# Order of the first loads and of the decay table in a fused retention and MoE kernel

## The chip, the cores and the metric

One Trainium2 chip, of which the kernel uses one core. The metric is the device time of one execution in microseconds, lower is better. A run is timed several times, and the median stands for it.

## What is computed

Three layers follow one another on 1536 rows (2 sequences of 768 tokens) of 512 numbers, all in float32:

- retention with 8 heads of 64 and one decay lam per head. In words: out[i] is the sum over j <= i of lam^(i-j) (q_i . k_j) v_j within a sequence. The reference works in blocks with a masked product inside a block and a state carried between blocks;
- a first MLP: `relu(x @ w_in)^2 @ w_out`, 512 to 2048 to 512;
- a second, gated MLP: `(sigmoid(x @ w_gate) * (x @ w_val)) @ w_out`, 512 to 1536 to 512.

## The kernel before

**Retention.** The sequences are cut into 12 chunks of 128 tokens (6 per sequence), which are worked in the order `ORDER` (L20). For each chunk, `att_scores` (L258) multiplies q and k on TensorE into PSUM; `att_prep` (L269) lets GpSimd (POOL) make `kd`, the keys times their decay, and from a sequence's second chunk on `qd`, the queries times the rows L, and lets VectorE (DVE) multiply the scores with the decay mask D into `at`, in two halves; `att_out` (L301) gives TensorE the state update (kd by v), the product with `at` (at by v), and the part from the carried state (qd by S); `att_state` (L335) and `att_x` (L347) take the results out on ScalarE (ACT) and VectorE. `att_decay` (L293) makes the decayed state on POOL.

**The decay table.** `powers` (L203) loads lam, lets POOL raise it to the powers 1 to 128 (W, L217), and stores a row of zeros with a one (Z) and then W into a small DRAM tensor `w_dram` over the scalar queue. `decays` (L223) reads that tensor back with shifted and overlapping addresses as the mask D (512 KB, in pieces of 512 bytes) and the rows L (two transfers of 128 KB), over the sync queue (SP). The last column of D is also the key decay that `kd` uses (L281).

**Weights.** Each weight unit (512 KB as it lies in DRAM) is loaded raw (`load_w`, L130), turned by ScalarE (`conv_act`, L140, two activations) and VectorE (`conv_dve`, L155, three operations) into float32, and stored back to DRAM for later. Each `conv_act` also issues the load of one more raw unit. A float32 product is made as three products of a high and a low part, for which `split_w` (L366) makes `whi` on ScalarE and `wlo` on VectorE.

**Order of the work.** Everything is written out by hand: each engine executes its instructions in program order, and waits between engines and for transfers are semaphores. The program loads FIRST, SIDE (over the scalar queue) and EARLY, in which "q0" is q and k of the first chunk in order, "v0" its k and v for the other products, "w" a raw weight unit and "D" the decay table. Then it issues the scores of the first UP = 4 chunks, prepares chunk 0 and runs a loop of LEAD = 7 passes (L815 to L833):

```python
for k, c in enumerate(order[:lead]):
    att_out(c)
    if UP <= k + 3 < lead:
        att_scores(order[k + 3])
    load(LOOP[k])
    ops = conv_dve()
```

A pass then prepares chunk k+1 and takes out chunk k, with the operations of one conversion woven between, and issues CONVS[k] calls of `conv_act`. After the passes `step_1` (L758) runs 16 times: a unit of the first MLP on the first 512 rows (`stage_a`, L406, through `mm_in`, and `stage_b`, L432, through `mm_out`), with up to PACE[f] conversions and the other five chunks in between. The rest of the kernel (the other 1024 rows by a Strassen scheme, and the second MLP) isn't touched. `warm_up` (L236) gives TensorE 44 small products at the start.

Of the kernel before, what the change touches and what calls it, by code (L numbers as in the profile page):

```python
# [7 lines left out]
F32 = mybir.dt.float32  # L8
# [4 lines left out]
P = 128  # L13
CH = 128
# [4 lines left out]

ORDER = (0, 6, 1, 2, 7, 3, 8, 4, 9, 5, 10, 11)  # L20
LEAD = 7
UP = 4
SLOTS = ((1, 3), (5, 8), (11, 13), (16, 19), (22, 25))


FIRST = "q0 q1 v0"
SIDE = "q2 q3"
EARLY = "D v1 w q4"
LOOP = ("v2 v3 q5", "q6 v4 v5 w", "v6 w v7", "q7", "", "", "")
RAW_BUFS = 4  # L30

CONVS = (1, 0, 1, 1, 1, 1, 0)
PACE = (2, 2, 2, 2, 2, 2, 2, 2, 2, 2, 2, 2, 2, 2, 1, 0)

MM = 0.2267
# [5 lines left out]
def retention_moe_kernel(  # L41
# [88 lines left out]
    def load_w(n):  # L130
        for _ in range(min(n, len(to_load))):
            ph, f, u = key = to_load.pop(0)
            t = wp.tile([P, 512, 2], I32, tag="w", name="raw")
            src = (w1 if ph == 1 else w2)[f, u].bitcast(I32)
            nc.sync.dma_start(out=t, in_=src.rearrange("p (n two) -> p n two", two=2))
            raw_t[key] = t

    ready = []

    def conv_act():  # L140

        if not to_conv or to_conv[0] not in raw_t:
            return
        key = to_conv.pop(0)
        t = raw_t.pop(key)
        j = unit("j")
        r = unit("r", I32)
        nc.scalar.activation(j, t[:, :, 1].bitcast(F32), AF.Copy, scale=2.0**-112)  # L150
        nc.scalar.activation(r, t[:, :, 0].bitcast(mybir.dt.uint32), AF.Copy, scale=2.0**-29)  # L151
        ready.append((key, j.bitcast(I32), r))
        load_w(1)

    def conv_dve():  # L155

        if not ready:
            return []
        key, j, r = ready.pop(0)
        ph, f, u = key  # L160
        m = unit("m", I32)
        w = unit("u")
        if ph == 1:
            w_t[key] = w

        def last():
            nc.vector.tensor_tensor(out=w.bitcast(I32), in0=m, in1=r, op=ALU.add)  # L167
            n_stored[0] += 1
            at(clock[0] + 4.0, lambda: nc.sync.dma_start(out=w32[ph][f, u], in_=w))

        return [
            lambda: nc.vector.tensor_scalar(
                out=m, in0=j, scalar1=3, scalar2=None, op0=ALU.logical_shift_left
            ),
            lambda: nc.vector.scalar_tensor_tensor(  # L175
                out=m, in0=j, scalar=-(2**31), in1=m, op0=ALU.bitwise_and, op1=ALU.bitwise_or
            ),
            last,
        ]
# [8 lines left out]
    def run(ops):  # L188
        weave(ops, [])
# [9 lines left out]
    L = const.tile([P, 4, CH], F32, name="L")  # L199
    S = [const.tile([P, 4, 64], F32, name=f"S{i}", tag=f"S{i}") for i in range(2)]  # L200
    w_dram = dram.tile([H, 256], F32, name="w_dram")

    def powers():  # L203


        src = bass.AP(lam.tensor, lam.offset, [[1, H], [0, 16], [1, 1]])
        nc.sync.dma_start(out=lam_sb, in_=src)
        nc.vector.memset(warm, 0.0)
        nc.gpsimd.iota(exi, pattern=[[1, 8]], base=0, channel_multiplier=8)
        nc.vector.memset(Z[:, 0:127], 0.0)  # L210
        nc.vector.memset(Z[:, 127:128], 1.0)
        nc.vector.tensor_scalar(
            out=exi, in0=exi, scalar1=127, scalar2=None, op0=ALU.bitwise_and
        )
        nc.vector.tensor_scalar(out=ex, in0=exi, scalar1=1.0, scalar2=None, op0=ALU.add)
        nc.scalar.dma_start(out=w_dram[:, 0:128], in_=Z)
        nc.gpsimd.tensor_tensor(out=W, in0=lam_sb.to_broadcast([P, 8]), in1=ex, op=ALU.pow)  # L217
        dst = w_dram[:]
        nc.scalar.dma_start(
            out=bass.AP(dst.tensor, dst.offset + 128, [[256, H], [8, 16], [1, 8]]), in_=W  # L220
        )

    def decays():  # L223


        src = w_dram[:]
        nc.sync.dma_start(
            out=D, in_=bass.AP(src.tensor, src.offset, [[1, P], [256, H], [1, CH]])
        )
        for r in range(2):  # L230
            nc.sync.dma_start(
                out=L[64 * r : 64 * r + 64],
                in_=bass.AP(src.tensor, src.offset + 256 * r + 128, [[0, 64], [512, 4], [1, CH]]),
            )
# [14 lines left out]
    def new_xr():  # L249
        for t in (1, 2):  # L250
            xr[t] = xp.tile([P, 4, TB], F32, tag=f"xr{t}", name=f"xr{t}")
# [17 lines left out]
    def att_prep(c):  # L269
        n = c % SEQ_CH  # L270
        sc = sc_t.pop(c)
        at_t[c] = double("at")
        dst = [pv(at_t[c][:, r, :]) for r in range(2)]
        qt = qk_t.pop(c)[:, 0, :]
        kn = kv_t[c][:, 0, :]
        if n < SEQ_CH - 1:
            kd = kd_t[c] = unit("kd")
            nc.gpsimd.tensor_tensor(  # L278
                out=kd.rearrange("s (h d) -> s h d", h=H),
                in0=kn.rearrange("s (h d) -> s h d", h=H),  # L280
                in1=D[:, :, CH - 1 : CH].to_broadcast([P, H, 64]), op=ALU.mult,  # L281
            )
        if n > 0:
            qd = qd_t[c] = unit("qd")
            nc.gpsimd.tensor_tensor(out=pv(qd), in0=pv(qt), in1=L, op=ALU.mult)  # L285
        return [
            lambda r=r: nc.vector.tensor_tensor(
                out=dst[r], in0=pv(sc[r]), in1=Dv[:, r], op=ALU.mult
            )
            for r in range(2)  # L290
        ]
# [431 lines left out]
    def load(what, eng=nc.sync):  # L723

        for x in what.split():
            if x == "w":
                load_w(1)
            elif x == "D":
                decays()
            elif x[0] == "q":  # L730
                load_qk(order[int(x[1:])], eng)
            else:
                load_kv(order[int(x[1:])], eng)
# [70 lines left out]

    with tc.manual_schedule():
        powers()
        load(FIRST)
        load(SIDE, nc.scalar)
        warm_up()
        load(EARLY)  # L810
        new_xr()
        for k in range(UP):
            att_scores(order[k])
        run(att_prep(order[0]))
# [6 lines that stand above are left out]
            if k + 1 < lead:  # L821
                weave(att_prep(order[k + 1]), ops[:2])
                run(att_state(c))
                att_decay(order[k + 1])
                weave(ops[2:], att_x(c))
            else:
                weave(split_w(1, 0), ops)
                rest.append(c)
            for m in range(CONVS[k]):
                if m:  # L830
                    run(conv_dve())
                conv_act()
            flush()  # L833


        keys = [(1, i, 0) for i in range(NF1 // 2)]
        prepare_a(keys[0], T1)
        at(T1 - 20.0, lambda: load_a((1, 1, 0)))
        combine_x([T1 + d for d in (-30, -25, -15, -13, -11, -9, -7, 2, 4, 6, 8)])
        for f in range(NF1):  # L840
            step_1(f)
        n_out = 24
        for k in range(n_out):
            convert(T2 + 1.0 + k * (T3 - T2 - 4.0) / n_out)
        for f in range(NF1):
            prepare_out(1, f, T2 + 24 * MM * f)
        uses = [use for i in range(NF1 // 2) for use in pair_in_1(i)]
        strassen(keys, uses, (None, lambda: close(1)))
        xc.clear()
        new_xr()  # L850
        for f in range(2):
            at(T3 - 24.0 + f, lambda f=f: load_units(2, f))
        at(T3 - 14.0, lambda: run(split_w(2, 0)))
        pair_out(1)


        for f in range(2, NF2):
            at(T3 + (36 * (f - 1) - 12) * MM - 8.0, lambda f=f: load_units(2, f))
        for k in range(3 * NF2 - n_out):
            convert(T3 + 2.0 + 3.6 * k)  # L860
        keys = [(2, i, u) for i in range(NF2 // 2) for u in range(2)]
        prepare_a(keys[0], T4)
        at(T4 - 20.0, lambda: load_a((2, 0, 1)))
        combine_x([T4 - 46.0 + 3.5 * k for k in range(11)])
        for f in range(NF2):
            step_2(f)
        for f in range(NF2):
            prepare_out(2, f, T5 + 24 * MM * f)
        uses = [use for i in range(NF2 // 2) for use in pair_in_2(i)]
        strassen(keys, uses, (None, lambda: close(2)))  # L870
        pair_out(2)
        flush()
        assert not agenda and not to_conv and not ready
# [62 lines left out]
```

## Time and profile before

| | |
|---|---|
| median of 3 runs | 601.86 us (600.67 to 604.19) |
| span of the profiled execution | 599.4 us; the page has no other time of it |
| TensorE busy | 582.6 us, 97% of the span, 3076 matmuls |
| VectorE busy | 448.6 us, 75% |
| ScalarE busy | 332.5 us, 55% |
| POOL busy | 36.9 us, 6% |
| DMA | 127.19 MB, mean 212 GB/s |
| granted TensorE clock | 0.993 of full speed, mean |

The span goes from the first to the last instruction. The profile names engines PE (TensorE matmul), PEld (its weight loads, beside PE), DVE, ACT, POOL and SP; a "q" behind the name (SPq, ACTq) is the sequencer that issues transfers. DMA queue q1 holds the transfers that SP issues, q10 those that ScalarE issues; both run on the same 16 DMA engines. In a timeline, "[0.40 <-DVE wlo L374]" says that the engine stood for 0.40 us before the instruction, until line 374's result was there. Work on an engine that is not the bottleneck costs nothing as long as it is done in time.

### The profile page before, as it was taken

To read this page: it belongs to the slowest core of one execution; us is meant where nothing else is said; L and a number is where in the kernel's file an instruction comes from. 1 tells how busy PE (TensorE), PEld (TensorE's weight loads), DVE (VectorE), ACT (ScalarE), POOL (GpSimd) and SP (SyncE) were. 2 spreads that over 40 slices of the span, in tenths; PEclk is the share of its full clock that TensorE was granted. 3 is DMA by queue.
4 is the path that set the end of the run, shared out by engine and by line. 5 is a ranking of instruction groups with operands and counts; after the bars stand their busy time and mean duration, and the time that the engine had idled before them with its cause. 6 is when DMAs were issued, how large, how long until landed. Compare 5 with 4: busy or idle time off the path is not lost.

```text
span 599.4 us, 8496 instructions
## 1 busy us (share of the span) xinstructions
PE 582.6 (97%) x3076; PEld 478.8 (80%) x3076; DVE 448.6 (75%) x673; ACT 332.5 (55%) x525; POOL 36.9 (6%) x34
## 2 busy tenths in 40 slices
PE   7799999999899999999999999999999999999997
PEld 7677878887678888888888888888888888888885
DVE  0699998999888868988877788694778787569101
ACT  0367787988556456756557654554464455537101
POOL 1672212100000000000000000000000000000000
PEclk9899999999999999999999999999999999999999
DMA  7996898682145377999978945511332422658003
GB/s 212 402 418 232 306 309 331 237 297 87 57 121 208 107 240 271 408 414 415 410 276 279 312 170 172 163 50 54 122 106 106 140 81 80 209 187 357 0 1 141
DMA packets 53578, 127.19 MB, mean 212 GB/s; under 512 B 5784, under 2 KB 7584, under 8 KB 53536
## 3 DMA queue, kind: packets, MB, share of 16 engines
q1 hardware_dynamic: 52376, 124.41, 57.9%
q10 hardware_dynamic: 1160, 2.24, 1.1%
q8 instruction: 24, 0.39, 0.3%
q14 instruction: 18, 0.15, 0.1%
HBM read 90.96 MB, written 35.66 MB: 211 GB/s over the span
## 4 chain that ended last, share of the span: by engine, by line
PE 87%; DVE 4%; DMA 2%; POOL 2%; issue 2%; ACT 1%; SPq 0%; ACTq 0%; POOLq 0%; DVEq 0%
PE p L545 30%; PE p L695 25%; PE p L386 17%; PE p L400 12%; DMA kv<-in_kv 1%; POOL kd L278 1%; PE p L329 1%; PE p L322 1%; POOL qd L285 1%; DMA lam_sb<-in_lam 1%; PE p L264 1%; DVE wlo L374 1%; DVE al L526 1%; DVE m L175 1%; ACT ah L520 1%
## 5 line engine op out<-in xcount | busy, mean ns | idle before, releaser
L545 PE MATMUL p<-xcl,ah 128*128 128x512 f32 x280 | 109.1, 390 | 2.5 <-DVE xcl L469 2.5
L545 PE MATMUL p<-xch,ah 128*128 128x512 f32 x280 | 109.4, 391 | 0.4 <-ACT s L554 0.2
L545 PE MATMUL p<-xch,al 128*128 128x512 f32 x280 | 109.0, 389 | 0.0
L695 PE MATMUL p<-g2h,whi 128*128 128x512 f32 x224 | 87.1, 389 | 0.0
L695 PE MATMUL p<-g2l,whi 128*128 128x512 f32 x224 | 87.1, 389 | 0.0
L695 PE MATMUL p<-g2h,wlo 128*128 128x512 f32 x224 | 87.1, 389 | 0.0
L545 PEld LDWEIGHTS p<-xcl,ah 128*128 128x128 f32 x280 | 52.6, 188 | 13.5 <-DVE xcl L469 2.9
L545 PEld LDWEIGHTS p<-xch,ah 128*128 128x128 f32 x280 | 52.5, 188 | 12.9 <-ACT s L554 1.4
L545 PEld LDWEIGHTS p<-xch,al 128*128 128x128 f32 x280 | 52.6, 188 | 11.0
L559 DVE TENSOR_TENSOR c<-p,s 128x512 f32<-128x512 f32 x60 | 41.2, 688 | 25.3 <-PE p L545 21.4
L554 ACT COPY s<-p 128x512 f32<-128x512 f32 x60 | 35.0, 586 | 37.4 <-PE p L545 37.4
L167 DVE CUSTOM_DVE_ANT_0 u<-m,r 128x1024 uint16<-128x1024 uint16 x68 | 49.5, 728 | 2.7
L374 DVE TENSOR_TENSOR wlo<-u,whi 128x512 fp32r<-128x512 f32 x68 | 46.1, 707 | 7.0 <-ACT whi L372 5.7
L150 ACT ACTIVATE j<-raw 128x512 f32<-128x512 f32 x68 | 45.6, 671 | 10.2 <-issue 5.3
L175 DVE SCALAR_TENSOR_TENSOR m<-j,m 128x512 int32<-128x512 int32 x68 | 49.5, 728 | 1.2
L151 ACT ACTIVATE r<-raw 128x512 int32<-128x512 uint32 x68 | 45.2, 665 | 8.7 <-PE p L695 5.5
L695 PEld LDWEIGHTS p<-g2l,whi 128*128 128x128 f32 x224 | 42.0, 188 | 8.8
L695 PEld LDWEIGHTS p<-g2h,whi 128*128 128x128 f32 x224 | 42.0, 188 | 8.7
L695 PEld LDWEIGHTS p<-g2h,wlo 128*128 128x128 f32 x224 | 42.0, 188 | 8.7
L372 ACT CAST whi<-u 128x512 fp32r<-128x512 f32 x68 | 39.0, 616 | 13.7 <-DVE u L167 13.2
L386 PE MATMUL p<-xh,wlo 128*128 128x512 f32 x160 | 43.2, 392 | 1.1 <-DVE wlo L374 1.1
L386 PE MATMUL p<-xh,whi 128*128 128x512 f32 x160 | 43.8, 395 | 0.0
(87 smaller groups left out, 911.6 us busy)
## 6 DMA issues: line engine op xcount, KB each, us to landing
raw<-in_w SPq DMA_DIRECT2D x68, 512.0 KB, 7.1
w<-u SPq DMA_DIRECT2D x68, 256.0 KB, 4.0
u<-w SPq DMA_DIRECT2D x64, 256.0 KB, 5.5
g<-g SPq DMA_DIRECT2D x56, 256.0 KB, 4.4
g<-g SPq DMA_DIRECT2D x28, 512.0 KB, 7.5
a<-w SPq DMA_DIRECT2D x20, 512.0 KB, 4.3
kv<-in_kv SPq DMA_DIRECT2D x12, 512.0 KB, 8.6
qk<-in_qk SPq DMA_DIRECT2D x10, 512.0 KB, 5.7
```

Of the source, the lines that this page charges most:

```text
L150: nc.scalar.activation(j, t[:, :, 1].bitcast(F32), AF.Copy, scale=2.0**-112)
L151: nc.scalar.activation(r, t[:, :, 0].bitcast(mybir.dt.uint32), AF.Copy, scale=2.0**-29)
L167: nc.vector.tensor_tensor(out=w.bitcast(I32), in0=m, in1=r, op=ALU.add)
L175: lambda: nc.vector.scalar_tensor_tensor(out=m, in0=j, scalar=-(2**31), in1=m, op0=ALU.bitwise_and, op1=ALU.bitwise_or),
L372: nc.scalar.copy(hi, src)
L374: lambda lo=lo, src=src, hi=hi: nc.vector.tensor_tensor(out=lo, in0=src, in1=hi, op=ALU.subtract)
L386: nc.tensor.matmul(acc, lhsT=a[:, kk * P : (kk + 1) * P], rhs=b[:, kk, :], start=i == 0, stop=i == 11,)
L400: nc.tensor.matmul(acc[e], lhsT=a[:, e * P : (e + 1) * P], rhs=b, start=first and i == 0, stop=last and i == 2,)
L545: nc.tensor.matmul(acc, lhsT=w[:, col, kk * P : (kk + 1) * P], rhs=x[:, kk, :], start=start and i == 0, stop=stop and i == 5, skip_group_c ...
L554: nc.scalar.copy(s, acc)
L559: nc.vector.tensor_tensor(out=c, in0=acc, in1=s, op=ALU.add)
L695: nc.tensor.matmul(acc[e, t], lhsT=a[:, e * P : (e + 1) * P], rhs=b[:, t, :], start=first and i == 0, stop=last and i == 2,)
```

## The change

It reorders what is loaded and done before the passes:

- SIDE, EARLY and the "D" of the load lists go; FIRST and NEXT load, all over SP, two raw weights as second and third, then the chunks in turn. LOOP holds the other loads, one raw weight or two in each pass; `conv_act(False)` no longer issues one.
- lam is loaded a second time, over the scalar queue, with all eight values on each partition (`lam8`). POOL raises them to the powers 0 to 127, one per partition (`KD`); DVE sets the first partition to 1. `kd` uses KD in place of D's last column.
- `decays` becomes `decay_table` (D) and `decay_rows` (L), both issued on the scalar queue: D between the two early `conv_act`, L behind the second. Both early `conv_dve` stand ahead of the first chunk's masks in VectorE's order.
- UP goes from 4 to 3, so that the fourth chunk's scores are issued in pass 0. CONVS moves the conversions of passes 0 and 2 on: passes 2 to 6 have one each.

```diff
--- before.py
+++ after.py
@@ -19,17 +19,15 @@
 
 ORDER = (0, 6, 1, 2, 7, 3, 8, 4, 9, 5, 10, 11)
 LEAD = 7
-UP = 4
+UP = 3
 SLOTS = ((1, 3), (5, 8), (11, 13), (16, 19), (22, 25))
 
 
-FIRST = "q0 q1 v0"
-SIDE = "q2 q3"
-EARLY = "D v1 w q4"
-LOOP = ("v2 v3 q5", "q6 v4 v5 w", "v6 w v7", "q7", "", "", "")
-RAW_BUFS = 4
-
-CONVS = (1, 0, 1, 1, 1, 1, 0)
+FIRST = "q0 w w q1 v0 q2 v1"
+NEXT = "q3 v2 q4 v3 w"
+LOOP = ("q5 v4 w", "q6 v5 w", "v6 w", "w q7", "v7 w", "w", "w")
+
+CONVS = (0, 0, 1, 1, 1, 1, 1)
 PACE = (2, 2, 2, 2, 2, 2, 2, 2, 2, 2, 2, 2, 2, 2, 1, 0)
 
 MM = 0.2267
@@ -137,7 +135,7 @@
 
     ready = []
 
-    def conv_act():
+    def conv_act(more=True):
 
 
 
@@ -150,7 +148,8 @@
         nc.scalar.activation(j, t[:, :, 1].bitcast(F32), AF.Copy, scale=2.0**-112)
         nc.scalar.activation(r, t[:, :, 0].bitcast(mybir.dt.uint32), AF.Copy, scale=2.0**-29)
         ready.append((key, j.bitcast(I32), r))
-        load_w(1)
+        if more:
+            load_w(1)
 
     def conv_dve():
 
@@ -199,6 +198,10 @@
     L = const.tile([P, 4, CH], F32, name="L")
     S = [const.tile([P, 4, 64], F32, name=f"S{i}", tag=f"S{i}") for i in range(2)]
     w_dram = dram.tile([H, 256], F32, name="w_dram")
+    lam8 = const.tile([P, H], F32, name="lam8")
+    exk = const.tile([P, 1], I32, name="exk")
+    exf = const.tile([P, 1], F32, name="exf")
+    KD = const.tile([P, H, 1], F32, name="KD")
 
     def powers():
 
@@ -206,6 +209,9 @@
         src = bass.AP(lam.tensor, lam.offset, [[1, H], [0, 16], [1, 1]])
         nc.sync.dma_start(out=lam_sb, in_=src)
         nc.vector.memset(warm, 0.0)
+        src = bass.AP(lam.tensor, lam.offset, [[0, P], [1, H]])
+        nc.scalar.dma_start(out=lam8, in_=src)
+        nc.gpsimd.iota(exk, pattern=[[1, 1]], base=0, channel_multiplier=1)
         nc.gpsimd.iota(exi, pattern=[[1, 8]], base=0, channel_multiplier=8)
         nc.vector.memset(Z[:, 0:127], 0.0)
         nc.vector.memset(Z[:, 127:128], 1.0)
@@ -213,22 +219,30 @@
             out=exi, in0=exi, scalar1=127, scalar2=None, op0=ALU.bitwise_and
         )
         nc.vector.tensor_scalar(out=ex, in0=exi, scalar1=1.0, scalar2=None, op0=ALU.add)
+        nc.vector.tensor_scalar(out=exf, in0=exk, scalar1=0.0, scalar2=None, op0=ALU.add)
         nc.scalar.dma_start(out=w_dram[:, 0:128], in_=Z)
         nc.gpsimd.tensor_tensor(out=W, in0=lam_sb.to_broadcast([P, 8]), in1=ex, op=ALU.pow)
         dst = w_dram[:]
         nc.scalar.dma_start(
             out=bass.AP(dst.tensor, dst.offset + 128, [[256, H], [8, 16], [1, 8]]), in_=W
         )
-
-    def decays():
+        nc.gpsimd.tensor_tensor(
+            out=KD[:, :, 0], in0=lam8, in1=exf.to_broadcast([P, H]), op=ALU.pow
+        )
+        nc.vector.memset(KD[0:1], 1.0)
+
+    def decay_table():
 
 
         src = w_dram[:]
-        nc.sync.dma_start(
+        nc.scalar.dma_start(
             out=D, in_=bass.AP(src.tensor, src.offset, [[1, P], [256, H], [1, CH]])
         )
+
+    def decay_rows():
+        src = w_dram[:]
         for r in range(2):
-            nc.sync.dma_start(
+            nc.scalar.dma_start(
                 out=L[64 * r : 64 * r + 64],
                 in_=bass.AP(src.tensor, src.offset + 256 * r + 128, [[0, 64], [512, 4], [1, CH]]),
             )
@@ -278,7 +292,7 @@
             nc.gpsimd.tensor_tensor(
                 out=kd.rearrange("s (h d) -> s h d", h=H),
                 in0=kn.rearrange("s (h d) -> s h d", h=H),
-                in1=D[:, :, CH - 1 : CH].to_broadcast([P, H, 64]), op=ALU.mult,
+                in1=KD.to_broadcast([P, H, 64]), op=ALU.mult,
             )
         if n > 0:
             qd = qd_t[c] = unit("qd")
@@ -725,8 +739,6 @@
         for x in what.split():
             if x == "w":
                 load_w(1)
-            elif x == "D":
-                decays()
             elif x[0] == "q":
                 load_qk(order[int(x[1:])], eng)
             else:
@@ -805,10 +817,15 @@
     with tc.manual_schedule():
         powers()
         load(FIRST)
-        load(SIDE, nc.scalar)
         warm_up()
-        load(EARLY)
+        load(NEXT)
         new_xr()
+        conv_act(False)
+        decay_table()
+        conv_act(False)
+        decay_rows()
+        run(conv_dve())
+        run(conv_dve())
         for k in range(UP):
             att_scores(order[k])
         run(att_prep(order[0]))
@@ -829,7 +846,7 @@
             for m in range(CONVS[k]):
                 if m:
                     run(conv_dve())
-                conv_act()
+                conv_act(False)
             flush()
 
 
```

## Rows read from the trace of the kernel before

**Rows 1.** Windows: start:end, length, busy time of each engine, PEclk, DMA share, GB/s.

```profile
0.00:50.00 50.00, 41.14 (x503) 34.49 (x504) 30.75 (x50) 18.59 (x32) 25.92 (x26) 0.93 0.94 346
15.00:20.00 5.00, 3.04 (x36) 2.44 (x33) 2.48 (x4) 0.37 (x1) 1.78 (x2) 0.50 1.06 369
```

**Rows 2.** Timeline of PE, 0 to 50 us: start, length, instruction, idle before.

```profile
6.98 3.61 PE L264 MATMUL p<-qk 64*128 64x128 f32 x32 [1.12 <-DMA qk<-in_qk]
...
13.43 1.87 PE L264 MATMUL p<-qk 64*128 64x128 f32 x16 [0.23 <-DMA qk<-in_qk]
17.26 1.13 PE L314 MATMUL p<-kv,kd 128*64 128x64 f32 x16 [1.96 <-POOL kd L278]
18.17 1.92 PE L322 MATMUL p<-at,kv 128*64 128x128 f32 x16
...
22.16 1.09 PE L322 MATMUL p<-at,kv 128*64 128x128 f32 x16 [1.04 <-ACT S L342]
23.19 1.16 PE L264 MATMUL p<-qk 64*128 64x128 f32 x16
24.54 0.69 PE L314 MATMUL p<-kv,kd 128*64 128x64 f32 x16 [0.19 <-POOL kd L278]
...
41.42 1.20 PE L386 MATMUL p<-xh,whi 128*128 128x512 f32 x4
...
47.41 1.20 PE L386 MATMUL p<-xh,wlo 128*128 128x512 f32 x4 [0.40 <-DVE wlo L374]
```

**Rows 3.** Timeline of DVE, 0 to 50 us.

```profile
16.18 2.48 DVE L287 TENSOR_TENSOR at<-p,D 128x512 f32<-128x512 f32 x4 [14.80 <-DMA D<-w_dram]
...
28.59 0.68 DVE L287 TENSOR_TENSOR at<-p,D 128x512 f32<-128x512 f32 x1
...
41.98 0.67 DVE L374 TENSOR_TENSOR wlo<-u,whi 128x512 fp32r<-128x512 f32 x1
42.58 0.41 DVE L172 TENSOR_SCALAR m<-j 128x512 int32<-128x512 int32 x1
```

**Rows 4.** Waits of the SP queue, 0 to 80 us: total, times, longest.

```profile
SPq L227 <- DMA w_dram<-W: 6.5, 1, 6.5
...
SPq L113 <- DMA D<-w_dram: 1.4, 1, 1.4
```

**Rows 5.** Timeline of the SP queue, 0 to 30 us.

```profile
1.60 0.87 SPq L113 DMA_DIRECT2D qk<-in_qk  x2
...
9.49 0.39 SPq L227 DMA_DIRECT2D D<-w_dram  x1
...
22.89 0.33 SPq L117 DMA_DIRECT2D kv<-in_kv  x1
24.12 0.33 SPq L135 DMA_DIRECT2D raw<-in_w  x1
```

**Rows 6.** Timeline of ScalarE and its queue, 0 to 30 us.

```profile
7.04 0.69 ACTq L219 DMA_DIRECT2D w_dram<-W  x1
7.77 1.47 ACTq L113 DMA_DIRECT2D qk<-in_qk  x2
9.27 1.28 ACT L342 ACT_TABLE_LOAD   x1 [9.27 <-issue]
...
21.75 0.35 ACT L342 COPY S<-p 128x256 f32<-128x256 f32 x1
```

**Rows 7.** DMA queues from 7.1 to 8.7 us: packets, MB, share.

```profile
q1 hardware_dynamic: 180, 0.65, 99.5%
```

**Rows 8.** DMA queues from 8.7 to 9.1 us.

```profile
q10 hardware_dynamic: 136, 0.00, 18.3%
```

**Rows 9.** DMA queues from 9 to 12 us.

```profile
q10 hardware_dynamic: 233, 0.89, 92.9%
q1 hardware_dynamic: 1, 0.00, 0.0%
```

**Rows 10.** Timeline of POOL, 0 to 25 us.

```profile
5.37 1.64 POOL L217 TENSOR_TENSOR W<-lam_sb,ex 128x8 f32<-128x8 f32 x1 [4.40 <-DMA lam_sb<-in_lam]
```

## Prediction

> **What bounds the kernel now.** I read the windows first. TensorE (PE) is idle 16.8 us of the 599.4 us span, and 8.9 us of that lie in the first 50 us [rows 1]; behind that PE has work without a break for long stretches. So the change can win only by an earlier start of that unbroken work, and it loses one for one what delays it. In the PE timeline [rows 2] this work begins with the first expert matmul at 41.42 us and is solid from 47.41 us. What to see ahead of it: the scores of chunk 0 run at 6.98, as soon as q0 lands, but nothing after the fourth scores (13.43) can run until the decay table is there.
>
> Next the VectorE (DVE) timeline [rows 3]: the first masked product at 16.18 ends an idle stretch of 14.80 us that D's landing ended. From 28.59 to 41.98 DVE has no gap: its work (masks, states, four conversions) paces the last passes. So the lead is a chain: D lands (16.1), 25.3 us of chunk work, first expert matmul. D's landing is the lever.
>
> Why D lands at 16.1: the SP queue stood 6.5 us until W (the powers) had landed in DRAM, and issued D at 9.49 [rows 4, 5]. Later loads issue at 22.89 and 24.12, each when one ahead has landed: a 512 KB transfer takes 1.22 us when the DMA engines are full [rows 5]. In [rows 4] SP's q5 also waits 1.4 us for D's landing: it is the eighth transfer from D on (L, L, v1, w, q4, v2, v3 between), so at most eight transfers are in flight, over both queues together, and the ninth waits where it is issued.
>
> **How the two queues share** is the price that decides, and no stretch of this trace has a deep backlog on one queue and a small transfer on the other. The nearest rows: W was issued on the scalar queue at 7.04 [rows 6], yet from 7.1 to 8.7 only q1 (SP's) moves packets, 180 of them [rows 7]; the scalar queue's come from 8.7 to 9.1 (136: W's 128 and 8 signals) [rows 8], as v0, the last load issued ahead, runs out. The other way round, D was issued on SP at 9.49, but from 9 to 12 us q10 (scalar) moves 233 packets (q2, q3) and q1 one [rows 9]. Both times the later transfer went after all that had been issued earlier, on either queue. I take it that this holds with more ahead: order of issue.
> The Trainium skill ("DMA: Bandwidth & Descriptors", section "Queues, rings and completion order") says otherwise: each DMA engine takes turns between the queues that have work, a packet of some 9 to 17 descriptors at a time. The rows of 9 to 12 us [rows 9] speak against it, unless D's descriptors were not ready before q3's turn; by it the sum is that of the first rival.
>
> **The change, part by part.**
> - *Two raw weights ahead.* FIRST becomes seven loads (q0 w w q1 v0 q2 v1), NEXT five more, all on SP, which no longer stops for W. SP issues q0 at 1.6 and takes 0.43 us each; the last two need slots of the small first transfers, free by 5.2 (the W product starts at 5.37 when lam has landed [rows 10]). So seven loads are issued ahead of W at 7.04. q0 lands at 7.0, the seventh at 7.0 + 6 x 1.22 = 14.3.
> - *W* is behind them: it lands at 14.3 and not 9.4. (Bound below: 9.4, if it passes them.)
> - *D on the scalar queue* waits there for W, so it is issued at 14.3; ScalarE is held at this point, with the second conversion and both L issues queued behind it. That conversion (two activations, some 0.7 each by the 0.35 of a copy of half the columns [rows 6]) runs by 17 and its DVE half by 19, ahead of the first mask in DVE's order and still before D; L follows D on its queue, and the first qd needs it some 7 us after D. SP itself waits for D only where a load takes D's slot, eight transfers on. By then SP has filled the slots again: eight less D's and one being turned over, 6 loads (bounds 4 and 7), done at 14.3 + 6 x 1.22 = 21.6. Before, D landed 2.7 us after q3, the transfer ahead of it (13.4 [rows 2] to 16.1), its 512 B pieces included; so now at 24.3 (21.9 to 25.5). **Term 1: 24.3 - 16.1 = +8.2** (+5.8 to +9.4).
> - *Key decay from KD.* A second power of 1.65 us like W's on POOL [rows 10], 7.0 to 8.7, ahead of v0's landing near 12: nothing. lam8, one iota, one small DVE operation and a memset lie in idle time: nothing. kd of chunks 0 to 2 no longer waits for D: the first uv leaves the path after D (17.26 to 18.17, 0.9 us).
> - *UP 4 to 3* puts one scores block (16 matmuls, 1.16 at full clock, 1.87 at half [rows 2]) behind D. The granted clock was 0.50 from 15 to 20 us, its lower level of 1.2 GHz, after PE had stood for most of 10.6 to 13.4 [rows 1]; I leave it so after the longer stand.
> - *Conversions moved.* Passes 0 and 1 hold none: before, ScalarE's conversion delayed the state copy to 21.75 [rows 6], for which PE stood 1.04 us at 22.16 [rows 2]. From D's landing to the uv of chunk 2 PE took 24.54 - 16.1 = 8.4 us. Now: the first half of the mask 0.8 (2.48 / 4 and the way to PE), ov 1.92 (at half clock), scores 1.5 (between the two clocks), uv 0.7, ov 1.09, scores 1.16: 7.2 [rows 2]. **Term 2: -1.2** (0 to -2, if the kd waits of 0.2 to 0.4 go too). The four conversions in the DVE stretch from 28.59 stay: nothing. The two early ones run on ScalarE and DVE in time in which both waited for D (14.80 us on DVE): nothing.
> - *One conversion is left over* for the first expert step, woven ahead of its low parts: one DVE operation of 0.41 (like the one at 42.58 [rows 3]) before the wlo that PE waited for at 47.41, up to 1.75 for all three (0.41 and two like the wlo, 0.67). **Term 3: +0.5** (0 to 1.75). Cover gone here means PE waits, as it did.
> - *Two more raws in the lead* (ten for eight): 2.4 us of DMA time; v3 to v6 land 1.2 to 2.4 later against loads, but chunk work now starts 8 us later: nothing. Two conversions fewer in the steps, where PE never waits: nothing.
>
> Sum: 8.2 - 1.2 + 0.5 = +7.5. The span becomes 606.9; the page gives no time of this execution around the span, and the median of the runs, 601.86, lies 2.5 above it: **609.4, say 609**, in its own range 606.5 to 611.
>
> **Rivals.**
> 1. *The queues take turns.* W then lands by 10.4, and D is issued when its slot is free, eight transfers back: at v0's or v1's landing, 11.9 to 14.3. It starts up to 1.7 later (W: 7.04 to 8.7 [rows 6, 8]), then stand one to four turns of SP loads (1.2 to 4.9), then 2.7: D lands at 17.5 to 23.6. With -0.7 of terms 2 and 3: +0.7 to +6.8, middle +3.7: 605.6. For it: separate queues. Against: [rows 7 to 9]. Chance 0.28.
> 2. *Hidden anyway*: D lands between 16.1 and 19, for a lighter backlog than I count, and the gain in passes 0 and 1 pays for it: 601 to 604. Chance 0.13.
> 3. *Faster: D at once.* If ScalarE's issue is served without a queue and no slot holds it, D goes out after the first conversion, near 10.4 (table load 1.28 [rows 6] after 7.8, then 1.4), starts 1.7 later and lands 2.7 after that, at 14.8: -1.3, with terms 2 and 3 -2.0, and up to -4 if it starts at once and the kd waits go: 598 to 600, middle 599. It decides from a landing before 16.8 on (16.1 + 0.7). For it: SP's stop of 6.5 us is gone. Against: the slot rule of [rows 4], for ScalarE's issue comes behind twelve loads. Chance 0.13.
>
> **How the numbers follow.** Order of issue has 0.46. A measurement of this kernel can tell about 0.5%, 3 us, from no change. Slower by more: all of the 0.46 and 0.6 of rival 1's 0.28 (above +3 in +0.7 to +6.8): 0.63. Faster by more: half of rival 3: 0.07. The rest: 0.30. The range leaves out the lower part of rival 3 and the top of the forecast (seven loads ahead and term 3 at its bound): 600.5 to 611.
>
> **What would show it.** Right: W landing past 13 us, D's wait on DVE ending past 21, the first expert matmul at 47 to 50, ScalarE standing at the D issue. Steps wrong: packets of q10 among q1's while SP has loads queued (rival 1); the first mask before 16.8 (rival 3); conversions on DVE later than D (then the weights, not the table, bound the lead). The whole is wrong if the expert matmuls begin by 42 or if PE stalls elsewhere than before them.

## The result, and the profile after

The change makes the kernel slower: 610.84 us (median of 4 runs, 609.82 to 611.54) against 601.39 us for the kernel before in the same comparison (600.67 to 604.19). The ratio is 1.014 (as recorded, not the quotient of the two medians), with a 95% interval of 1.0114 to 1.0165. That is "slower by over 0.5%", to which the forecast gave 0.63; the time lies 1.8 us above the predicted 609.0 and inside the range, close to its upper end of 611. The profiled execution has a span of 609.6 us, 10.2 more than before, and a mean granted clock of 0.977 (0.993 before). All of it is in the lead.

**Where the chain goes.** These lines are from the chain of waits of the kernel after (start, length, what), from its first instruction to the first masked product:

```profile
5.97 1.65 POOL W L224
7.64 7.39 DMA w_dram<-W
15.05 9.86 DMA D<-w_dram
...
25.01 0.70 DVE at L301
```

W is stored at 7.64 and lands after 7.39 us; D is issued that moment and lands after 9.86. Together they are 17.3 us of the lead. Before, W was issued at 7.04 [rows 6] and D's wait ended at 16.18 [rows 3]. POOL starts on W at 5.97, not 5.37 [rows 10], and so W is issued 0.6 later.

**What W and D stand behind.** SP's queue (start, length, line) shows the loads issued around them; lam, q0, w, w, q1, v0 and q2 come before the first of these lines:

```profile
7.25 0.33 SPq L115 DMA_DIRECT2D kv<-in_kv  x1
8.54 0.33 SPq L111 DMA_DIRECT2D qk<-in_qk  x1
11.11 0.33 SPq L115 DMA_DIRECT2D kv<-in_kv  x1
15.04 0.33 SPq L111 DMA_DIRECT2D qk<-in_qk  x1
```

Seven loads are out when W is issued, as forecast, and SP sends a further one when the transfer whose slot it takes has landed. The DMA queues (packets, MB, share of 16 engines) in six stretches, 7.7 to 11.4, 11.5 to 14.5, 15 to 17.8, 17.9 to 18.9, 20.9 to 21.9 and 23 to 25 us, one group for each in this order:

```profile
q1 hardware_dynamic: 428, 1.56, 102.8%
...
q1 hardware_dynamic: 346, 1.22, 101.0%
q10 hardware_dynamic: 136, 0.00, 2.5%
...
q1 hardware_dynamic: 310, 1.14, 101.0%
...
q10 hardware_dynamic: 295, 0.15, 87.3%
q1 hardware_dynamic: 30, 0.06, 18.7%
...
q1 hardware_dynamic: 93, 0.34, 85.9%
q10 hardware_dynamic: 93, 0.05, 15.3%
...
q10 hardware_dynamic: 358, 0.17, 37.6%
q1 hardware_dynamic: 13, 0.02, 6.4%
```

For 3.7 us after W's issue, and for 2.8 us after D's, the scalar queue (q10) moves nothing at all, as in [rows 7]. Then both queues move packets at once: W's small ones spread over 3 us among 346 of SP's; D's first have the engines almost to themselves (295 to 30), then they alternate with SP's loads, 93 to 93, and only behind those does the rest come. A 512-byte packet for each 4096-byte one is a poor bargain: D lands behind the three loads (q4, v3, w) that were issued beside it at 15.04 to 15.89. From 23 us on it isn't the loads that hold it: both queues together move only 0.19 MB in 2 us, nearly all of it the scalar queue's. Why this end is so slow isn't shown.

SP itself stands, first for W and then for D. Two lines of its waits, 0 to 80 us (total, times, longest), which answer to [rows 4]:

```profile
SPq L111 <- DMA D<-w_dram: 8.6, 1, 8.6
...
SPq L111 <- DMA w_dram<-W: 3.6, 1, 3.6
```

The first of these is the stand before SP's next load, at 24.93: it waits for D's slot, the fifth transfer issued after D and not the eighth. The second is the stand before the load at 15.04, for W's own slot. Between W's landing and D's, SP so sends only three loads.

**What waits for D.** VectorE's timeline (start, length, instruction, idle before):

```profile
25.01 2.48 DVE L301 TENSOR_TENSOR at<-p,D 128x512 f32<-128x512 f32 x4 [6.79 <-DMA D<-w_dram]
```
And TensorE's:

```profile
25.75 2.56 PE L336 MATMUL p<-at,kv 128*64 128x128 f32 x16 [8.93 <-DVE at L301]
28.25 2.08 PE L278 MATMUL p<-qk 64*128 64x128 f32 x16
30.26 1.12 PE L328 MATMUL p<-kv,kd 128*64 128x64 f32 x16
31.85 1.09 PE L336 MATMUL p<-at,kv 128*64 128x128 f32 x16 [0.47 <-ACT S L356]
...
33.97 0.69 PE L328 MATMUL p<-kv,kd 128*64 128x64 f32 x16
...
48.56 0.43 PE L336 MATMUL p<-at,kv 128*64 128x128 f32 x2 [0.99 <-DVE at L301]
49.49 1.09 PE L336 MATMUL p<-at,kv 128*64 128x128 f32 x14 [0.50 <-DVE at L301]
...
51.53 1.19 PE L400 MATMUL p<-xh,whi 128*128 128x512 f32 x4
```

The line at 25.01 is the one at 16.18 in [rows 3], 8.8 us later. TensorE stands 8.93 us for it, and its first expert matmul comes at 51.53 where [rows 2] had 41.42: 10.1 later, and the span ended 10.2 later. Nothing behind it gives anything back.

The clock is the second thing to see (windows: start:end, length, busy time of PE, PEld, DVE, ACT, POOL, then PEclk, DMA share, GB/s); the first line answers to [rows 1], where PE had 41.14 us of work in the first 50 us and not 33.05:

```profile
0.00:50.00 50.00, 33.05 (x440) 28.30 (x442) 23.10 (x42) 13.88 (x24) 22.61 (x25) 0.76 0.90 330
15.00:20.00 5.00, 1.82 (x24) 1.41 (x22) 1.81 (x3) 1.61 (x3) 2.60 (x2) 0.50 1.04 357
20.00:25.00 5.00, 0.00 (x0) 0.00 (x0) 0.00 (x0) 0.00 (x0) 0.00 (x0) 0.50 0.80 263
25.00:30.00 5.00, 4.25 (x32) 3.61 (x32) 3.51 (x6) 0.59 (x1) 4.09 (x4) 0.50 0.82 255
30.00:35.00 5.00, 4.53 (x78) 3.82 (x78) 2.05 (x4) 0.96 (x2) 0.00 (x0) 0.82 1.00 395
```

From 15 to 30 us the granted clock is 0.50 of full speed, the lower level of 1.2 GHz, through the long stand and 5 us beyond it. The first `at` product takes 2.56 us (1.92 in [rows 2]), the fourth scores 2.08 and the next uv (the state update, kd by v) 1.12. The 2.56 isn't the clock's alone: the product starts at 25.75 with the first half of its mask and gets the second half 0.6 us later, as VectorE makes four such halves, two for each of two chunks, in 2.48.

### The profile page after: what moved, and what is told of

Its sections match the earlier page's. It is cut to its first block, busy times and chain, and to the rows that moved or that the text cites. A ratio compares the mean times of both kernels' runs of the same rounds, so it can differ in the third digit from the quotient of the medians.

```text
span 609.6 us, 8526 instructions
## 1 busy us (share of the span) xinstructions
PE 585.4 (96%) x3076; PEld 481.4 (79%) x3076; DVE 448.1 (74%) x675; ACT 333.0 (55%) x525; POOL 36.8 (6%) x36
## 3 DMA queue, kind: packets, MB, share of 16 engines
q10 hardware_dynamic: 2600, 1.98, 1.1%
## 4 chain that ended last, share of the span: by engine, by line
PE 89%; DVE 5%; DMA 4%; ACT 1%; issue 1%; POOL 0%; ACTq 0%; DVEq 0%; POOLq 0%
PE p L559 31%; PE p L709 25%; PE p L400 17%; PE p L414 12%; DMA D<-w_dram 2%; PE p L336 2%; PE p L278 1%; DMA w_dram<-W 1%; PE p L343 1%; DVE u L166 1%; DMA lam_sb<-in_lam 1%; DVE m L174 1%; DVE at L301 1%; DVE m L171 1%; PE p L328 0%
## 5 line engine op out<-in xcount | busy, mean ns | idle before, releaser
L174 DVE SCALAR_TENSOR_TENSOR m<-j,m 128x512 int32<-128x512 int32 x68 | 48.0, 707 | 1.3
L400 PE MATMUL p<-xl,whi 128*128 128x512 f32 x160 | 42.8, 389 | 0.0
```

Source lines behind the costliest of these rows:

```text
L174: lambda: nc.vector.scalar_tensor_tensor(out=m, in0=j, scalar=-(2**31), in1=m, op0=ALU.bitwise_and, op1=ALU.bitwise_or),
L400: nc.tensor.matmul(acc, lhsT=a[:, kk * P : (kk + 1) * P], rhs=b[:, kk, :], start=i == 0, stop=i == 11,)
```

## The experiments

All of these compute the whole output; two add TensorE products on a tile of zeros that nobody reads. The kernel before ran beside them on each chip; its median was 601.4 to 603.1 us, so ratios are compared, not times.

**Is it the scalar queue?** First the table goes back to SP, at the same place of the changed program:

```diff
 def decay_table():
...
-        nc.scalar.dma_start(
+        nc.sync.dma_start(
             out=D, in_=bass.AP(src.tensor, src.offset, [[1, P], [256, H], [1, CH]])
...
 def decay_rows():
...
-            nc.scalar.dma_start(
+            nc.sync.dma_start(
                 out=L[64 * r : 64 * r + 64],
```

> The changed kernel with D and L issued on SP again, at the same place in the program. Theory (SP's backlog delays W and then D): W still lands near 15.0, because seven loads are ahead of it; but D then stands in line on SP instead of taking turns with SP's loads: it is issued at 15.1 with some two loads ahead, starts near 17.4 and lands at 20 to 21 instead of 24.9. Time about 606 to 607, 4 less than the changed kernel's 610.8. Rival (the raw weights and the early conversions ahead of the masks are the cause): nothing changes, 610 to 611. Rival (the scalar queue alone is the cause): back to 601 to 602.

Ratio 1.0123 (1.0081 to 1.0165), as with the scalar queue. SP's queue in this run:

```profile
12.36 0.33 SPq L133 DMA_DIRECT2D raw<-in_w  x1
15.04 0.39 SPq L238 DMA_DIRECT2D D<-w_dram  x1
```
And the first masked product on VectorE:

```profile
24.81 2.48 DVE L301 TENSOR_TENSOR at<-p,D 128x512 f32<-128x512 f32 x4 [9.90 <-DMA D<-w_dram]
```

D is issued at 15.04, and its wait ends at 24.81, 0.2 from the changed kernel's. All twelve loads have been issued by then, the last at 12.36, and SP stands until W has landed. Queue q1 moves 599 packets (2.20 MB, more than four loads) between 15 and 20.4 us, and the 512-byte pieces of D and L come after them (1554 packets, 0.88 MB, from 20.5 to 23, most of them these pieces). On one queue it is order of issue; on two it is a late start and then sharing; the landing is nearly the same. The expectation of 606 to 607 is a miss, and the theory that the scalar queue alone makes the loss falls.

The opposite test: the kernel before, with only its D and L issued on the scalar queue.

```diff
 def decays():
...
-        nc.sync.dma_start(
+        nc.scalar.dma_start(
             out=D, in_=bass.AP(src.tensor, src.offset, [[1, P], [256, H], [1, CH]])
...
-            nc.sync.dma_start(
+            nc.scalar.dma_start(
                 out=L[64 * r : 64 * r + 64],
```

> The kernel before with only D and L moved to the scalar queue. Theory: SP no longer stands for W and fills its slots with v1, w, q4 and more, W starts some 3 us after its issue and takes turns with them, D is issued behind q2 and q3: W lands at 11 to 14, D past 21, time 606 to 611. Rival (raw weights and early conversions are the cause): 601 to 602.

Ratio 1.0001 (0.9976 to 1.0025): W's landing came as expected, D's landing and the time did not. ScalarE's queue in this run:

```profile
6.83 0.70 ACTq L219 DMA_DIRECT2D w_dram<-W  x1
...
11.74 0.39 ACTq L227 DMA_DIRECT2D D<-w_dram  x1
```
And the first masked product on VectorE:

```profile
17.25 2.48 DVE L287 TENSOR_TENSOR at<-p,D 128x512 f32<-128x512 f32 x4 [15.87 <-DMA D<-w_dram]
```

SP no longer stops for W, so v1 and a weight go out first, and W lands at 11.7 and not near 9.4. D takes 5.4 us from its issue (6.6 on SP before) and is 1.1 us later than before, for W was. With a short list ahead of it the scalar queue takes no longer from D's issue to its landing than SP did.

**Is it the raw weights and their early conversions?** They are taken out of the changed kernel; the chunk loads keep their places:

```diff
-FIRST = "q0 w w q1 v0 q2 v1"
-NEXT = "q3 v2 q4 v3 w"
+FIRST = "q0 q1 v0 q2 v1"
+NEXT = "q3 v2 q4 v3 w w w"
...
-CONVS = (0, 0, 1, 1, 1, 1, 1)
+CONVS = (1, 1, 1, 1, 1, 1, 1)
...
-        conv_act(False)
         decay_table()
-        conv_act(False)
         decay_rows()
-        run(conv_dve())
-        run(conv_dve())
```

> The changed kernel without the two raw weights ahead (they go to the end of NEXT) and without the two early conversions (CONVS has one in each pass). Theory: SP still fills its slots with loads ahead of W and D, only with other loads; W lands past 13, D past 22, time 608 to 612. Rival (raw weights and early conversions): 600 to 603.

Ratio 1.0102 (1.006 to 1.0143), as expected. The first masked product on VectorE:

```profile
23.45 2.48 DVE L301 TENSOR_TENSOR at<-p,D 128x512 f32<-128x512 f32 x4 [14.15 <-DMA D<-w_dram]
```

W lands at 15.0 as in the changed kernel, for SP has simply sent other loads ahead, and D's wait ends at 23.45, 1.6 earlier. So it isn't the weights as such: seven chunk loads ahead of W do nearly the same.

**Is it the key decay?** The kernel before, with lam8, KD and the new `kd` alone:

```diff
+        src = bass.AP(lam.tensor, lam.offset, [[0, P], [1, H]])
+        nc.scalar.dma_start(out=lam8, in_=src)
...
+        nc.gpsimd.tensor_tensor(
+            out=KD[:, :, 0], in0=lam8, in1=exf.to_broadcast([P, H]), op=ALU.pow
+        )
+        nc.vector.memset(KD[0:1], 1.0)
...
-                in1=D[:, :, CH - 1 : CH].to_broadcast([P, H, 64]), op=ALU.mult,
+                in1=KD.to_broadcast([P, H, 64]), op=ALU.mult,
```

> The kernel before with only the key decay from KD. Theory: D lands as before (16.1), the first uv moves ahead of it, 0.9 us at most comes off the chain: 600.5 to 601.4, a gain too small to be sure of. Rival (the second power or the second load of lam delays W): W half a us to 1.7 us later and the time with it, 602 to 603.

Ratio 1.0029 (1.0005 to 1.0052): a small loss where I had costed nothing. D lands as before (16.05), so what is lost lies behind it. TensorE's timeline:

```profile
17.39 1.09 PE L334 MATMUL p<-at,kv 128*64 128x128 f32 x16
20.68 0.69 PE L326 MATMUL p<-kv,kd 128*64 128x64 f32 x16 [2.20 <-POOL kd L290]
22.36 1.98 PE L334 MATMUL p<-at,kv 128*64 128x128 f32 x16 [1.00 <-ACT S L354]
24.27 1.80 PE L276 MATMUL p<-qk 64*128 64x128 f32 x16
```

The first `at` product runs 0.8 us earlier than in [rows 2], but then TensorE stands 2.20 us for the second `kd`, whose uv comes 0.3 later than before (20.39), and 1.00 for the state copy, as before (1.04). Behind these stands the products run slower (1.98 and 1.80 where [rows 2] had 1.09 and 1.16). The uv of chunk 2 comes at 26.00 (24.54 before). The same run shows the price of lam8: W's store is issued at 7.54, half a microsecond later, as two loads of lam now start together. The scalar-queue experiment without lam8 has it at 6.83.

**Is it the list ahead of the table?** Everything of the change stays, but D and L go on SP directly behind the first five loads, and no other load passes them:

```diff
-FIRST = "q0 w w q1 v0 q2 v1"
-NEXT = "q3 v2 q4 v3 w"
+FIRST = "q0 w w q1 v0"
+NEXT = "q2 v1 q3 v2 q4 v3 w"
...
         warm_up()
+        decay_table()
+        decay_rows()
         load(NEXT)
         new_xr()
         conv_act(False)
-        decay_table()
         conv_act(False)
-        decay_rows()
```

> The changed kernel with everything kept (raw weights as second and third load, early conversions, KD, UP 3) but D and L issued on SP directly behind five loads (q0 w w q1 v0), so that SP stands there until W has landed; the other loads follow. Theory (the number of loads issued ahead of W and D is the cause, whatever they are): W lands near 12 in place of 15.0, D finds the DMA engines free, lands at 15 to 17 in place of 24.9, time 600.5 to 603. Rival (raw weights, early conversions ahead of the masks, KD or the scores moved behind D): stays at 607 to 611.

Ratio 1.0054 (1.0036 to 1.0072), 604.0 us of span. The first masked product on VectorE:

```profile
16.30 2.48 DVE L301 TENSOR_TENSOR at<-p,D 128x512 f32<-128x512 f32 x4 [1.38 <-DMA D<-w_dram]
```
And TensorE's timeline:

```profile
19.68 2.08 PE L278 MATMUL p<-qk 64*128 64x128 f32 x16 [6.47 <-DMA qk<-in_qk]
...
22.59 1.92 PE L336 MATMUL p<-at,kv 128*64 128x128 f32 x16
...
46.58 1.20 PE L400 MATMUL p<-xh,whi 128*128 128x512 f32 x4
```

D's wait ends at 16.30, where [rows 3] had 16.18. W lands at 12.4 behind the five, D is issued there with nothing large ahead of it, and lands when it did before, with the raw weights and the early conversions still in place. With the table on SP alone D was as late as in the change, so it is the place that does it: this shows the list ahead of W and D as the cause of D's lateness. At the first expert matmul it gives back 5.0 of the 10.1 us (51.53 to 46.58). The other 5 are a new wait. TensorE has the third scores ahead of the first `at` product, q2 was the sixth load and now stands behind D, and PE waits 6.47 us for it. The DMA engines are full in the lead (their share from 15 to 30 us is 1.03 or more in this run), so what D gains q2 loses, as long as two raw weights (2.4 us) are in front. The expected 600.5 to 603 held for D and not for the time.

So the same without the weights: q0 q1 v0 q2 v1 ahead of the table, nothing early, the rest as in the change.

```diff
-FIRST = "q0 w w q1 v0 q2 v1"
-NEXT = "q3 v2 q4 v3 w"
+FIRST = "q0 q1 v0 q2 v1"
+NEXT = "q3 v2 q4 v3 w"
...
         warm_up()
+        decay_table()
+        decay_rows()
         load(NEXT)
...
-        conv_act(False)
-        decay_table()
-        conv_act(False)
-        decay_rows()
-        run(conv_dve())
-        run(conv_dve())
```

> As the run with five loads ahead of the table, but the five are q0 q1 v0 q2 v1: no raw weight ahead and no early conversion; KD, UP 3 and five conversions from pass 2 on stay. Theory of what that run has left (the raw weights put q2 behind D and L, and the third scores, which stand ahead of the first ov on TensorE, wait for q2 until 19.7): D lands near 16.2 again, the third scores run at 11 to 12, the first ov at 17, the first expert matmul near 41, ratio to the kernel before 0.997 to 1.001. Rival (KD, the scores behind D or the conversion left over cost the remainder): ratio 1.004 to 1.006 as with the raw weights.

Ratio 1.003 (1.0011 to 1.0048), between the theory's range and the rival's. The first masked product on VectorE:

```profile
16.23 2.48 DVE L301 TENSOR_TENSOR at<-p,D 128x512 f32<-128x512 f32 x4 [6.96 <-DMA D<-w_dram]
```
And TensorE's timeline:

```profile
16.97 2.57 PE L336 MATMUL p<-at,kv 128*64 128x128 f32 x16 [2.75 <-DVE at L301]
...
42.18 1.20 PE L400 MATMUL p<-xh,whi 128*128 128x512 f32 x4
```

The first expert matmul comes 0.8 after [rows 2]. The late D and the wait for q2 are gone, and with them most of the loss. What is left is of the size of the key decay alone (1.0029), but the key decay wasn't taken out of this run. The expert matmul's time and the end of the span don't go together to better than a microsecond: here the span, 601.4, is 2.0 longer than before.

Over all runs, D's issue, which is W's landing, came at 9.2 to 9.9 us with three loads issued ahead of W, 11.7 to 12.4 with five and 15.0 with seven. That is the size of the list, whatever is on it, and whichever queue issues D.

**Is it the clock?** The changed kernel with 65 more of the small warm-up products ahead of the first `at` product, to keep TensorE busy while it stands:

```diff
         for k, c in enumerate(order[:lead]):
+            if k == 0:
+                warm_up(65)
             att_out(c)
```

> The changed kernel with 65 small products on zeros on TensorE in front of the first att_out, where it stands for D. Theory of the remainder (D is 8.9 late, the first expert matmul 10.1, because TensorE is at its lower clock from 8 to 32 us): the granted clock is 1.0 at 25 us, the first ov takes 1.1 in place of 2.6 and the fourth scores 1.2 in place of 2.1; time 607.5 to 609, 2 to 3 less than the change. Rival (the remainder is DVE's or POOL's): 610 to 611.

Ratio 1.0111 (1.0066 to 1.0155), which can't be told from the change's 1.014; the span is 2.0 us shorter. Windows as above:

```profile
15.00:20.00 5.00, 4.99 (x89) 4.62 (x87) 1.81 (x3) 1.26 (x2) 2.61 (x2) 0.96 1.03 350
20.00:25.00 5.00, 0.00 (x0) 0.00 (x0) 0.40 (x1) 0.37 (x1) 0.00 (x0) 0.72 0.82 267
25.00:30.00 5.00, 4.56 (x48) 3.89 (x48) 3.52 (x7) 0.58 (x1) 4.09 (x4) 0.60 0.89 311
```

The products ended at 19.3; the clock was 0.96 while they ran, 0.72 in the next 5 us and 0.60 after the stand. D's wait ended 0.4 earlier (24.60), and from D's landing to the uv of chunk 2 TensorE took 0.8 us less. So some 0.8 us of the loss goes with the clock; how much more a clock held to the end would give back isn't shown, for these products ended 5 us before D came. The expectation (clock 1.0 at 25 us, 607.5 to 609) is a miss.

**Can the parts be put in an order that wins?** With three loads ahead of the table and none of the early conversions (D and L on SP):

```diff
-FIRST = "q0 w w q1 v0 q2 v1"
-NEXT = "q3 v2 q4 v3 w"
+FIRST = "q0 q1 v0"
+NEXT = "q2 v1 q3 v2 q4 v3 w w w"
...
-CONVS = (0, 0, 1, 1, 1, 1, 1)
+CONVS = (1, 1, 1, 1, 1, 1, 1)
...
         warm_up()
+        decay_table()
+        decay_rows()
         load(NEXT)
```

> As the run without early raws, but D and L on SP directly behind three loads (q0 q1 v0), then q2 v1 and the rest. Theory: W lands near 10, D at 14 to 15, but the third scores wait for q2 at 16; time 599.5 to 602. Compared with the run without early raws (609.4) only the place of D differs. Rival (what keeps that run slow is KD, UP 3 or a conversion in every pass): 607 to 610.

Ratio 1.0071 (1.0045 to 1.0097), though D's wait ended at 13.97, 2.2 before [rows 3]; the time, 607.43, fell into the rival's range. TensorE stood 6.14 us for q2's scores and then, at 26.62, 1.98 for a state copy on ScalarE, which was held by the conversion of pass 0, whose raw weight was late. Then only two scores ahead of the first `at` product, UP and the look-ahead both at 2:

```diff
-UP = 3
+UP = 2
...
-            if UP <= k + 3 < lead:
-                att_scores(order[k + 3])
+            if UP <= k + 2 < lead:
+                att_scores(order[k + 2])
```

> A candidate: as with three loads ahead of the table, but two scores ahead and the others two passes ahead of their use (UP 2), so that nothing waits for q2 in front of the first masked product. Theory: D lands at 14 to 15 and the first ov starts 0.7 later; the next bound is v1, two loads behind L, near 18: time 599 to 601, the lowest so far by 1 to 2. Rival (v1 and the clock take it back): 601 to 603.

Ratio 1.0046 (1.0023 to 1.0069). The expected 599 to 601 was missed again (605.92). The first `at` product ran at 14.99, but a state copy behind the same late conversion now cost 3.04 us, at 26.56. So, last, the conversions of passes 0 and 1 go as well, as in the change (CONVS 0, 0, 1, ...), and lam8 is loaded behind W's store:

```diff
-UP = 3
+UP = 2
...
-FIRST = "q0 w w q1 v0 q2 v1"
-NEXT = "q3 v2 q4 v3 w"
+FIRST = "q0 q1 v0"
+NEXT = "q2 v1 q3 v2 q4 v3 w"
...
-        src = bass.AP(lam.tensor, lam.offset, [[0, P], [1, H]])
-        nc.scalar.dma_start(out=lam8, in_=src)
         nc.gpsimd.iota(exk, pattern=[[1, 1]], base=0, channel_multiplier=1)
...
             out=bass.AP(dst.tensor, dst.offset + 128, [[256, H], [8, 16], [1, 8]]), in_=W
         )
+        src = bass.AP(lam.tensor, lam.offset, [[0, P], [1, H]])
+        nc.scalar.dma_start(out=lam8, in_=src)
```

> The candidate with two scores ahead, mended: conversions from pass 2 on (in the first form ScalarE stood in pass 0 for a raw weight with the state copy behind it, 3 us of TensorE), one raw weight in place of three ahead, and lam's second load behind W's store. Theory: D lands near 13.8, first ov near 14.7, v1 and q2 near 17, second ov near 19.5, first expert matmul at 39 to 41: ratio 0.994 to 0.999. Rival (the lower clock takes it back): 1.000 to 1.003.

Ratio 0.9977 (0.9964 to 0.9991): 601.21 us beside 602.57, the one version that beats both kernels, by 1.4 us, less than 0.5% but with an interval below 1. Which of its edits brings it past the version before wasn't tried. The first masked product on VectorE:

```profile
13.01 2.49 DVE L301 TENSOR_TENSOR at<-p,D 128x512 f32<-128x512 f32 x4 [0.73 <-DMA D<-w_dram]
```
And TensorE's timeline:

```profile
18.91 0.69 PE L328 MATMUL p<-kv,kd 128*64 128x64 f32 x16 [0.97 <-POOL kd L292]
...
23.00 0.69 PE L328 MATMUL p<-kv,kd 128*64 128x64 f32 x16 [1.24 <-POOL kd L292]
...
40.04 1.19 PE L400 MATMUL p<-xh,whi 128*128 128x512 f32 x4
```

D is issued at 9.17 (9.49 in [rows 5]), but only three loads went ahead of it and q2, q3 come behind it, so its wait ends at 13.01, 3.2 us earlier. Of these 3.2 the first expert matmul keeps 1.4 (40.04): the uv products now wait for the `kd` of their chunks (0.97 and 1.24), whose v loads are behind the table. The profiled span is 599.4, no shorter than before, so that the gain rests on the medians. Thirty more small products in TensorE's stand ahead of the first `at` product gave nothing that can be told:

```diff
         for k, c in enumerate(order[:lead]):
+            if k == 0:
+                warm_up(30)
             att_out(c)
```

> The mended candidate with 30 products on zeros on TensorE between the second scores and the first att_out, in time in which it stands for D. Theory (the clock after the stand is part of the cost): granted clock 1.0 from 10 to 17 us, first ov 1.1 in place of 2.1 to 2.6, 0.5 to 1.5 us off the mended candidate: ratio 0.992 to 0.998. Rival (v1 and q2 land when they land): the same as the mended candidate within 0.2%.

Ratio 0.9993 (0.9979 to 1.0007): the expected 0.992 to 0.998 is a miss, and the rival, the same within 0.2%, holds.

## Why the prediction was right, and what in it was wrong

The direction and its cause (W and then D behind SP's loads) were right, and the size nearly (10.2 us of span for 7.5). By the steps of the prediction, in the profiled executions:

| step | forecast | measured |
|---|---|---|
| term 1, D's landing | +8.2 (16.1 to 24.3) | +8.8 (to 24.9) |
| term 2, D to the uv of chunk 2 | -1.2 (8.4 to 7.2) | +0.6 (9.06: 33.97 - 24.91) |
| from there to the first expert matmul | 0 | +0.7 (16.88 to 17.56) |
| term 3, left-over conversion | +0.5 | +0.1 (10.1 at the matmul, 10.2 at the end) |
| sum | +7.5 | +10.2 |

- **Term 1** was sized right, in part by luck. For W the rule, order of issue, gave the right landing: 15.0 for 14.3, with the seventh load, for which POOL's second `kd` waited until 15.00. Of the 0.7 too little, 0.3 is q0 (the first scores run at 7.28, for 6.98 before), and the loads took some 1.28 us each, not 1.22. W's own issue, 0.6 late through lam8, an edit that I costed at nothing, isn't shown to have moved its landing. For D the rule holds on one queue (the table on SP), but not over two: q10's packets did come among q1's while SP had loads queued, which was named as rival 1's sign. What takes its place is a start some 2.8 us after the issue, and then sharing. The "6 loads" were not there: SP stood 3.6 us for W's slot and 8.6 for D's, which came five transfers on and not eight. From 15 to 25 us q1 moved some 2.3 MB, four to five loads; what was missing to six, some 2 us, the slow end from 23 to 25 made up for.
- **Rival 1** had the sharing, but its time (605.6) assumed that W lands by 10.4 (15.0) and that a transfer starts within 1.7 us of its issue (3.7 and 2.8). The Trainium skill ("DMA: Bandwidth & Descriptors", section "Queues, rings and completion order") has the queues take turns; this case's trace agrees from 20.9 to 21.9 us (93 packets to 93), but not in the 3.7 us behind W's issue, in which the scalar queue moved none. How many packets make a turn the rows don't show.
- **Rivals 2 and 3** fall: D landed at 24.9, past 19 and past 16.8. ScalarE stood 4.65 us at the D issue, as the prediction had it. The first expert matmul at 51.53 lies past the 47 to 50 named, by the terms below.
- **Term 2 had the wrong sign**, and this is the step that failed. I put ov (the `at` product) at 1.92, the scores "between the two clocks" at 1.5 and uv at 0.7; they took 2.50 and 2.01, start to start, and 1.12: 1.5 more. Of this, 0.9 is the scores and uv at the clock of 0.50, which held past 30 us. The other 0.6 is ov, and there it is the mask's second half: with five loads ahead of the table, where VectorE had finished the masks by 18.8, the same product at the low clock took 1.92 (22.59). The forecast counted the wait for the first half alone. That the length of the stand keeps the clock down isn't shown: with five chunk loads ahead the stand was 2.75 us, not 8.93, and the first three blocks behind it took as long (16.97, 19.47 and 21.48, the last for 1.12). A further 0.47 is a wait that the trace puts down to the state copy (31.85), which I took to be hidden once the conversions were gone; with the table on SP, the same product ran without it at 30.97, and why isn't shown.
- **The conversions that stay in VectorE's stretch**, costed at nothing, stand with 0.7, the two waits for `at` at 48.56 and 49.49 among it. It isn't shown that the move made them: the scalar-queue experiment, with CONVS as before, has the same waits of 1.00 and 0.50 in its last pass, and so has the key-decay one (0.98 and 0.50).
- **Term 3** was nearly nothing: no long wait for `wlo` shows. The early conversions were done on VectorE by 18.2, long before D, as the prediction had it.

The sum was 2.7 short and the time only 1.8, because the forecast added 2.5 for the median's distance from the span (1.2 for the changed kernel) and then rounded 609.4 down. That these errors partly cancel is luck; the time lies only 0.2 us inside the range.

## What to carry to other kernels

A small transfer on which a chain hangs has to be issued before the deep list of large loads, on whatever queue: here a queue of its own got neither W nor D past the loads that were already out. In a lead where the DMA engines are full, every load put in front delays the others by its own length, so count from the first use of each: here the table, then q2, then the raw weights. Weights brought and converted early showed no gain here (1.0054 with them, 1.003 without, five loads ahead of the table in both; the intervals overlap).

## What was not expected of the hardware

- A transfer on an idle queue, issued while the other queue had a backlog, moved no packet for 2.8 us (D) and 3.7 us (W), and then shared the engines with the other queue. In [rows 7, 8] the wait of 1.7 us looked like order of issue. W still landed only with the last load issued ahead of it.
- With the table on SP, nearly all of the 512-byte pieces of D and L were moved by 23 us, but D's wait ended only at 24.81. In the change the same tail stands from 23 to 25 us, with the engines less than half busy. Which DMA engine is late there, and why, isn't shown.
- Two small loads of lam at once made the first 0.5 to 0.9 us later (W's store at 7.5 to 7.6 with both, 6.7 to 7.0 with one or with the second behind).
- Behind a stand of 8.9 us, and behind one of 2.75 just as well, the granted clock was at its lower level for some 5 us of work; small products that ended 6 us before the work began again only partly helped (0.60).
